# A first product with seven products of quarters in four of its blocks, and gating shared with GpSimd

## The chip, the cores and the metric

The kernel runs on one core of a Trainium2 chip. The metric is the device time of one execution in microseconds; the number given for a kernel is the median of its runs.

## What is computed

A recurrent attention (a decaying state per head) is followed by a two-layer network with a gated non-linearity. Cut to what matters:

```python
# q, k, v: (B=4, H=8, S=768, D=64)
for t in range(S):
    state = gamma * state + outer(k[:, :, t], v[:, :, t])
    y[:, :, t] = q[:, :, t] @ state / sqrt(D)
x = y.transpose(0, 2, 1, 3).reshape(B * S, H * D)      # 3072 tokens, 512 features
h = x @ w_in                                           # 512 -> 2048
g = maximum(h, 0) + alpha * minimum(h, 0)              # alpha: one number per feature of h
out = g @ w_out                                        # 2048 -> 512
```

## The kernel before

**Blocks and units.** The 3072 tokens are worked through in six blocks n of 512 tokens (`TB`), each of two units u of 256 (`U`). While block n is in the two products of the network, units 2(n+1) and 2(n+1)+1 of the next block go through the attention. Everything is issued in an order written out by hand; the products are generators, and `tick(gen, m)` issues the next m of their matmuls between pieces of attention. Each engine works through its queue in that order.

**First product** (`ffn1`, L591 to L604). 2048 features are 16 tiles of 128. In blocks 2 to 5 a tile is four matmuls over the 512 input features, with 512 tokens as columns, into one PSUM bank (`hps`); the 16 tiles go in turn through all eight banks. ScalarE writes `hm` = relu(-h) (L602), and VectorE gates, `gt` = hm * (1 - alpha) + h (L604), reading the bank a second time. In blocks 0 and 1 some tiles are done in halves of 256 tokens.

**Second product.** Block 0 is a plain product (`ffn2`, L629). In blocks 1 to 5 `ffn2_seven` (L677) cuts it into two by two quarters and does seven products of quarters in place of eight (16 matmuls of 256 columns each), with sums of quarters of `gt` (`g_sums`, L575, four per block on VectorE) and of `w_out` (`w_sums`, L562, once). One bank is seeded: ScalarE copies the first product's bank `ox` into `oy` (L699), and TensorE adds to it. The first two sums of `gt` are made in halves, one half-way through the first product and one at its end (in blocks 2 to 5; whole at its end in block 1).

**Attention in a block** (n = 1 in one form, n = 2 to 4 in another with halves of units). GpSimd scales k and q and casts them (`rescale`, L178) and casts v (`cast_v`, L194); these two `rescale`s and the cast per unit stand in the queue at the start of a block, the first of them held until the last `g_sums` of the block before (`gate`, `behind`). DMA transposes give `kq`. TensorE makes the states (`halves_mm`), the scores (`half_mm`), VectorE masks the scores (`half_masks`, L349), VectorE and GpSimd advance the state (`middle` L294, `behind_middle` L305/L306, with casts L326, L442), TensorE makes the output of the heads (`halves_out`, L377, L391), and ScalarE writes it as `xT` (`take_y`, L546), which is x of the next block.

Where the next block starts, VectorE's queue holds: the last `g_sums`, the addition for one store (`plus`, L703), the addition for the last store of the block (which reads bank 0), and then the gates of the next block.

Tiles that aren't persistent come from pools with 1 to 3 buffers under a tag.

Of the kernel before, what the change touches and what calls it, by code (L numbers as in the profile page):

```python
# [14 lines left out]
MULT = mybir.AluOpType.mult  # L15
ADD = mybir.AluOpType.add
# [5 lines left out]
def kernel(  # L22
# [61 lines left out]
    mj = sbp.tile([128, 512], F16, tag="mj", name="mj")[:, 0:384]  # L84
# [3 lines left out]
    warm = sbp.tile([128, 128], FP, tag="warm", name="warm")[:, 0:1]  # L88
    oma_sb = sbp.tile([128, 128], FP, tag="oma", name="oma")[:, 0:NFT]
# [4 lines left out]
    wsum = sbp.tile([128, 4, HF, HM], F16, tag="wsum", name="wsum")  # L94

    def ps(bank, name, dt=FP, n=512):
        return psp.tile([128, n], dt, tag=f"b{bank}", name=name)
# [11 lines left out]
    moved, mids = {}, {}  # L109
# [177 lines left out]
    def middle(u, c):  # L287

        s = sums.pop((u, c))
        m = sbp.tile([128, NP, 64], FP, tag="tm", bufs=2, name=f"tm{u}_{c}")  # L290
# [7 lines left out]
    def behind_middle(ucms):  # L298
# [4 lines left out]
        ss = sbp.tile([128, NP, 64], FP, tag="ss", bufs=2, name=f"ss{u}_{c}")  # L303
        t = sbp.tile([128, NP, 64], FP, tag="tf", bufs=3, name=f"tf{u}_{c}")
# [42 lines left out]
    def half_masks(u, a):  # L347
        m2 = sbp.tile([128, 512], F16, tag=f"m2{a}{u % 2}", bufs=2, name=f"m2{a}")
        nc.vector.tensor_tensor(  # L349
            out=m2.rearrange("p (x i) -> p x i", x=8),  # L350
            in0=live[u][a].rearrange("p (x i) -> p x i", x=8),
            in1=mj[:, 256:320].unsqueeze(1).to_broadcast([128, 8, 64]),
            op=MULT,
        )
        live[u][a] = m2
# [50 lines left out]
    def state_sum(u, c, eng):  # L406
# [3 lines left out]
        t = sbp.tile([128, NP, 64], FP, tag="tf", bufs=3, name=f"tf{u}_{c}")  # L410
        if u % UPB == 0 and c == 0:
            nc.vector.tensor_tensor(out=t, in0=s, in1=dec, op=MULT)
        else:
            ss = sbp.tile([128, NP, 64], FP, tag="ss", bufs=2, name=f"ss{u}_{c}")
# [50 lines left out]
    def masks(u, hh, parts=(0, 1)):  # L465
        for a in parts:
            m2 = sbp.tile([128, 512], F16, tag=f"m2{a}{hh}", bufs=2, name=f"m2{a}{hh}")
# [86 lines left out]
    def w_sums(i, lo, hi, eng=nc.vector):  # L554

        w = w_out_all.rearrange("p (k f) (j e) -> p k f j e", k=2, j=2)
        w12, w21, w22 = w[:, 0, lo:hi, 1, :], w[:, 1, lo:hi, 0, :], w[:, 1, lo:hi, 1, :]
        t1, t2, t3, t4 = (wsum[:, x, lo:hi, :] for x in range(4))
        o, a, b = (
            (t1, w12, w[:, 0, lo:hi, 0, :]), (t2, w22, t1), (t3, w22, w12), (t4, w21, t2)  # L560
        )[i]
        return eng.tensor_tensor(out=o, in0=a, in1=b, op=SUB)  # L562
# [14 lines left out]
    def ffn1(n, banks, apart=0):  # L577
# [9 lines left out]
        for i, (f0, nf, lo, hi) in enumerate(turns):  # L587
# [12 lines left out]
            hm = sbp.tile([128, TB], FP, tag="hm", bufs=3, name="hm")  # L600
# [18 lines left out]

    def ffn2(n, banks, parts=1):  # L620
# [3 lines left out]
        for f0 in range(0, NFT, step):  # L624
            for tq in range(4):
                if f0 == 0:
                    opss[tq] = ps(banks[tq % len(banks)], "ops")
                for ft in range(f0, f0 + step):
# [7 lines left out]
                    if ft == NFT - 1:  # L636
                        tag = ("os", "cu")[tq % 2]
                        os_sb = sbp.tile([128, d_model], FP, tag=tag, bufs=3, name=tag)
# [7 lines left out]
    def ffn2_seven(n, x, y, z=None):  # L646
# [16 lines left out]
        def ws(i):  # L663
            return lambda f: wsum[:, i, f, :]
# [7 lines left out]

        def product(o, lhs, rhs, first, after=None):

            for m in range(2):
                for f in range(HF):
# [4 lines left out]
                        start=(first and f == 0 and m == 0),  # L681
                        stop=(f == HF - 1),
                        skip_group_check=True,
                    )
                    if f == HF - 1 and after is not None:
                        after(m)
                    if m == 0 or f < HF - 1:
                        yield

        def kept(o, name="cu"):  # L690
            t = sbp.tile([128, 2, HM], FP, tag=name, bufs=3, name=name)
            moves((t, [t[:, 0, :], t[:, 1, :]]), o)
            return t

        def moves(o, i):

            whole = o[0] is not None and i[0] is not None
            for a, b in [(o[0], i[0])] if whole else zip(o[1], i[1]):
                nc.scalar.activation(out=a, in_=b, func=COPY, bias=0.0, scale=1.0)  # L699

        def plus(o, t, name="os"):
            so = sbp.tile([128, 2, HM], FP, tag=name, bufs=3, name=name)
# [3 lines left out]
        def store(i, j, t):  # L706
# [367 lines left out]
```

## Time and profile before

| | |
|---|---|
| median of three runs | 201.17 us (199.87 to 201.18) |
| the profiled execution | 199.25 us, span 197.4 us |
| TensorE busy, its matmuls | 190.0 us (96%), 2493 |
| VectorE / ScalarE / GpSimd busy | 148.9 / 115.2 / 93.6 us |
| granted TensorE clock | 1.00 |
| 16 DMA engines, mean rate | 176 GB/s |

Times in a trace are counted from the span's start. A row of a timeline or of the chain begins with the start and the duration in microseconds; a group's row ends with its total busy time, the mean of one in nanoseconds, and the engine's idle time before it with what ended that. PE is TensorE, DVE VectorE, ACT ScalarE, POOL GpSimd, SP the engine that issues most transfers. The chain is followed back from the last instruction: at each step to what released it. TensorE's records overlap (a matmul of 512 columns is shown as 379 ns and the next starts 216 ns after it), so its pace is read from the chain.

### The profile page before, as it was taken

How to read it: one execution, taken by the hardware profiler on the slowest of the kernel's cores; microseconds unless marked ns; L12 is line 12 of the kernel's file. 1: busy time of each engine (PE TensorE's matmuls, PEld its weight loads, DVE VectorE, ACT ScalarE, POOL GpSimd, SP SyncE). 2: the span in 40 equal slices, each digit the busy share in tenths (PEclk: the TensorE clock that was granted, in tenths of full speed). 3: DMA queues.
4: the chain of work that ended last, by engine and by line, in shares of the span. 5: the costliest groups of instructions: out<-in, count | busy, mean ns of one | idle time of the engine just before them, and what ended most of it. 6: DMA issues, size and time to landing. Idle time of an engine off the chain costs nothing.

```text
span 197.4 us, 5972 instructions
## 1 busy us (share of the span) xinstructions
PE 190.0 (96%) x2493; PEld 125.3 (64%) x2493; DVE 148.9 (75%) x243; ACT 115.2 (58%) x200; POOL 93.6 (47%) x107
## 2 busy tenths in 40 slices
PE   6788999999999999999999999999999999999993
PEld 2456544577477788644788544888544888445882
DVE  6896985527789996489986489985589993789821
ACT  3467675257286667466477476377466485566221
POOL 6288047399439374960187950268940370000000
PEclk9999999999999999999999999999999999999999
DMA  6999999999899979898895999948955011200014
GB/s 159 335 259 169 202 260 260 294 181 188 200 228 124 327 160 278 224 262 183 197 233 123 309 193 212 240 111 201 253 108 128 9 56 58 104 0 3 0 53 159
DMA packets 88185, 34.75 MB, mean 176 GB/s; under 512 B 57936, under 2 KB 87648, under 8 KB 88160
## 3 DMA queue, kind: packets, MB, share of 16 engines
q1 hardware_dynamic: 83760, 30.16, 62.3%
q0 software_dynamic: 4224, 4.19, 13.5%
q8 instruction: 19, 0.31, 0.7%
q10 hardware_dynamic: 176, 0.04, 0.2%
q14 instruction: 6, 0.05, 0.1%
HBM read 27.31 MB, written 6.29 MB: 170 GB/s over the span
## 4 chain that ended last, share of the span: by engine, by line
PE 90%; DMA 6%; SPq 1%; ACT 1%; POOL 0%; issue 0%; POOLq 0%
PE hps L591 42%; PE ox L677 16%; PE oy L677 14%; PE ops L629 7%; DMA win<-in_moe_w_in_dram 3%; DMA vs<-in_v_dram 3%; SPq L158 1%; PE y L523 1%; PE trb L223 1%; PE oz L677 1%; PE st L277 1%; PE sca L456 1%; PE y L377 1%; PE ow L677 1%; PE y L391 1%; PE y L491 1%
## 5 line engine op out<-in xcount | busy, mean ns | idle before, releaser
L591 PE MATMUL hps<-xT,win 128*128 128x512 f16 (+1 forms) x448 | 84.7, 349 | 0.3 <-DMA win<-in_moe_w_in_dram 0.3
L604 DVE SCALAR_TENSOR_TENSOR gt<-hm,oma,hps 128x512 f16<-128x512 f32 (+1 forms) x112 | 70.7, 668 | 15.2 <-ACT hm L602 10.1
L602 ACT ACTIVATE hm<-hps 128x512 f32<-128x512 f32 x96 | 57.0, 597 | 31.6 <-PE hps L591 28.8
L591 PEld LDWEIGHTS <-win 128*128 128x128 f16 x448 | 43.5, 98 | 38.9 <-DMA win<-in_moe_w_in_dram 0.5
L677 PEld LDWEIGHTS <-gs 128*128 128x128 f16 x320 | 30.9, 98 | 3.9 <-DVE gs L575 0.3
L677 PEld LDWEIGHTS <-gt 128*128 128x128 f16 x240 | 22.8, 98 | 4.5
L178 POOL TENSOR_TENSOR kdq<-ks,tab 128x1024 f16<-128x1024 f32 (+1 forms) x12 | 19.4, 1614 | 10.5 <-DMA ks<-in_k_dram 7.9
L178 POOL TENSOR_TENSOR kdq<-qs,tab 128x1024 f16<-128x1024 f32 (+1 forms) x13 | 20.4, 1571 | 3.3 <-DVE wsum L562 3.0
L326 POOL CAST tg<-tm 64x256 f16<-64x256 f32 x12 | 4.8, 398 | 33.9 <-DVE tm L294 22.5
L677 PE MATMUL ox<-wout,gt 128*128 128x256 f16 x160 | 19.3, 273 | 0.0
L677 PE MATMUL oy<-wsum,gs 128*128 128x256 f16 x160 | 19.1, 273 | 0.0
L546 ACT ACTIVATE xT<-y 128x512 f16<-128x512 f32 x23 | 15.7, 742 | 3.9 <-PE y L523 2.8
L703 DVE TENSOR_TENSOR os<-ox,cu 128x512 f32<-128x512 f32 x8 | 5.5, 692 | 13.4 <-PE ox L677 12.1
L629 PE MATMUL ops<-wout,gt 128*128 128x512 f16 x64 | 15.3, 380 | 0.0
L194 POOL CAST vx<-vs 128x1024 f16<-128x1024 f32 (+1 forms) x13 | 12.5, 973 | 3.9 <-DMA vs<-in_v_dram 3.9
L575 DVE TENSOR_TENSOR gs<-gt 128x1024 f16<-128x1024 f16 (+1 forms) x14 | 12.8, 918 | 0.3
L229 ACT ACTIVATE kq<-trb 128x1024 f16<-128x1024 f16 x8 | 8.2, 1023 | 6.5 <-PE trb L223 6.4
L306 POOL TENSOR_TENSOR tf<-ss,tab 128x256 f32<-128x256 f32 x10 | 10.3, 1030 | 2.5 <-DVE ss L305 1.3
L699 ACT ACTIVATE cu<-oy 128x512 f32<-128x512 f32 (+1 forms) x12 | 6.3, 526 | 8.3 <-PE oy L677 7.7
L416 POOL TENSOR_TENSOR tf<-ss,tab 128x256 f32<-128x256 f32 x8 | 6.5, 817 | 9.8 <-DVE ss L415 9.8
L677 PE MATMUL oy<-wsum,gt 128*128 128x256 f16 x80 | 9.5, 272 | 0.1
L629 PEld LDWEIGHTS <-gt 128*128 128x128 f16 x64 | 5.8, 98 | 6.0
(86 smaller groups left out, 213.6 us busy)
## 6 DMA issues: line engine op xcount, KB each, us to landing
out_dram<-os SPq DMA_DIRECT2D x21, 256.0 KB, 3.5
ks<-in_k_dram SPq DMA_DIRECT2D x32, 128.0 KB, 3.7
qs<-in_q_dram SPq DMA_DIRECT2D x8, 512.0 KB, 5.1
vs<-in_v_dram SPq DMA_DIRECT2D x32, 128.0 KB, 4.4
ks<-in_k_dram SPq DMA_DIRECT2D x8, 256.0 KB, 4.5
qs<-in_q_dram SPq DMA_DIRECT2D x8, 256.0 KB, 4.6
win<-in_moe_w_in_dram POOLq DMA_DIRECT2D x4, 512.0 KB, 6.6
wout<-in_moe_w_out_dram POOLq DMA_DIRECT2D x4, 512.0 KB, 6.5
```

The lines of the kernel that those rows point to most:

```text
L178: return eng.tensor_tensor(out=kdq[:, t, :, h0:h1, :].rearrange("p r h d -> p h r d"), in0=staged[u]["kq"[t]][:, h0:h1, :].rearrange("p h ...
L194: eng.tensor_copy(out=o, in_=i)
L229: nc.scalar.activation(out=kq.rearrange("p (x a) i -> p x a i", x=4)[:, :, 2 * hh : 2 * hh + 2, :], in_=trb.rearrange("p (x a i) -> p x a ...
L306: nc.gpsimd.tensor_tensor(out=t, in0=ss, in1=dec, op=MULT)
L416: eng.tensor_tensor(out=t, in0=ss, in1=dec, op=MULT)
L546: nc.scalar.activation(out=o, in_=i, func=COPY, bias=0.0, scale=1.0,)
L575: return nc.vector.tensor_tensor(out=o, in0=a, in1=b, op=op)
L591: nc.tensor.matmul(out=hps[:, f, :].rearrange("p (u t) -> p u t", t=U), lhsT=w_in_all[:, hp, 128 * (f0 + f) : 128 * (f0 + f) + 128], rhs=x ...
L602: nc.scalar.activation(out=hm, in_=hps, func=RELU, bias=0.0, scale=-1.0)
L604: nc.vector.scalar_tensor_tensor(out=gt[:, f0 + f, U * lo : U * hi], in0=hm[:, f, :], scalar=oma_sb[:, f0 + f : f0 + f + 1], in1=hps[:, f, :],
L629: nc.tensor.matmul(out=opss[tq], lhsT=gt[:, ft, 128 * tq : 128 * tq + 128], rhs=w_out_all[:, ft, :], start=(ft == 0), stop=(ft == NFT - 1),)
L677: nc.tensor.matmul(out=o[1][m], lhsT=lhs(f, m), rhs=rhs(f), start=(first and f == 0 and m == 0), stop=(f == HF - 1), skip_group_check=True,)
```

## The change

1. *Seven products in the first product.* In blocks 2 to 5, tiles 6, 7, 14 and 15 (a two by two cut of features, tokens and input features) are done by seven products of quarters, "steps" 1 to 7, each four matmuls of 256 columns: step 1 makes a product in banks 2 and 3, ScalarE copies it into banks 0 and 1 (the seed), steps 6, 7 and 4 add to the seed, steps 5 and 3 go to bank 4; after steps 6 and 7 ScalarE copies the seed out, and after 4 and 3 VectorE adds such a copy to bank 4 into PSUM, where the usual gate reads it. They need four sums of `w_in` (`in_sums`, once, on GpSimd, after block 1's attention) and four of x (`x_sums`, in each block, on VectorE, right after the attention of the block before).
2. *The order* of tiles and steps is the list `PLAN`, and the twelve plain tiles go mostly through banks 7, 6 and 5 in turn.
3. *GpSimd gates* tiles 3, 5, 8 and 11: ScalarE copies the bank, GpSimd makes min(h, 0) * (alpha - 1), then adds h. It also masks one of each block's four score tiles, which ScalarE copies first.
4. *Sums of gated tiles*: the first two are made whole, after all tiles. Sum 3 is made earlier in the attention's order.
5. *Sums of w_out*: the first is made in place of a quarter of `w_out`, by VectorE, after block 0's second product; before, by GpSimd into a buffer of its own.
6. *Last block*: the seven products of the second product come in another order, with one more bank; what ends last is a VectorE addition of 128x256 in two halves, and two stores go out from ScalarE's queue.
7. *Buffers*: PSUM is one tile cut by bank, some pools become rings in fixed turn, masks have one buffer in place of two.

The core of the diff:

```diff
+    def x_sums(n, eng):
+        xs = sbp.tile([128, 4, 2, U], F16, tag="xs", name=f"xs{n}")
+        b11, b21, b12, b22 = (xT[n][:, ul, 2 * k : 2 * k + 2, :] for ul in range(2) for k in range(2))
+        t1, t2, t3, t4 = (xs[:, i] for i in range(4))
+        for o, a, b in ((t1, b12, b11), (t2, b22, t1), (t3, b22, b12), (t4, b21, t2)):
+            eng.tensor_tensor(out=o, in0=a, in1=b, op=SUB)
...
+    def prelu_pool(n, f, hps):
+        h = ring([128, TB], "hm", 4, "hm")
+        nc.scalar.activation(out=h, in_=hps, func=COPY, bias=0.0, scale=1.0)
+        m = sbp.tile([128, TB], FP, tag="hn", bufs=1, name="hn")
+        nc.gpsimd.tensor_scalar(
+            out=m, in0=h, scalar1=0.0, scalar2=al_sb[:, f : f + 1], op0=MIN, op1=MULT
+        )
+        nc.gpsimd.tensor_tensor(out=gts[n][:, f, :], in0=h, in1=m, op=ADD)
...
+    def ffn1_mixed(n, plan, banks, pool=()):
...
+            o, lhs, rhs, start = {
+                1: (f11, w(0, 0), x(0, 0), True),
+                2: (f11, w(1, 0), x(1, 0), False),
+                3: (bv, wi[:, 3], x(1, 1), False),
+                4: (g21, w(1, 1), xs[:, 3], False),
+                5: (bv, wi[:, 0], xs[:, 0], True),
+                6: (g21, wi[:, 1], xs[:, 1], False),
+                7: (g21, wi[:, 2], xs[:, 2], False),
+            }[i]
...
+            if i == 1:
+                nc.scalar.activation(out=g21, in_=f11, func=COPY, bias=0.0, scale=1.0)
+            elif i in (6, 7):
+                t = ring([128, 2, HM], "cu", 3, "cu")
+                nc.scalar.activation(out=t, in_=g21, func=COPY, bias=0.0, scale=1.0)
+                sums[f, i] = t
+            elif i in (3, 4):
+                o = (bf if i == 3 else bg)
+                nc.vector.tensor_tensor(
+                    out=o[:, :, U : 2 * U], in0=bv, in1=sums.pop((f, 6 if i == 3 else 7)), op=ADD
+                )
...
-    def half_masks(u, a):
+    def half_masks(u, a, eng=nc.vector):
...
+        if eng is nc.gpsimd:
+            nc.scalar.activation(out=m2, in_=i, func=COPY, bias=0.0, scale=1.0)
+            i = m2
...
-    w_sums(0, 0, HF, G)
...
+    w_sums(0, 0, HF)
     tick(half)
+    a = steps(6, 2, 0, 4)
+    PLAN = [0, 1, a[1], a[5], 2, a[6], a[2], 3, a[7], 4, a[4], 5, 8, a[3], 9, 10, 11, 12, 13]
+    PBANKS = (7, 6, 5, 7, 6, 5, 7, 6, 5, 1, 7, 4)
+    POOLED = (3, 5, 8, 11)
...
-            gen = ffn1(n, (7, 2, 3, 1, 0, 6, 5, 4, 7, 1, 0, 4, 5, 6, 7, 1))
+            gen = ffn1_mixed(n, *((PLAN, PBANKS, POOLED) if more else (PLAN, PBANKS, POOLED)))
...
             tick(gen)
+            g_sums(n, 0, GS if more else 0, HF)
+            g_sums(n, 1, GS if more else 0, HF)
...
             half_mm(u0, (4, 5))
+            half_masks(u0, 1, G)
             m00 = middle(u0, 0)
...
-            tick(gen, 9)
-            half_masks(u0, 1)
+            tick(gen, 1)
+            g_sums(n, 2, 0, HF)
             m10 = middle(u1, 0)
...
             halves_out(u1, (4, 5))
             state_copy(s11, part=1)
+            x_sums(n + 1, V)
...
             out_mm(u0 + 1, (4, 5))
+            for i in range(4):
+                in_sums(6, i, G)
+            x_sums(n + 1, V)
```

228 lines of the change are left out of this document (170 added, 58 removed).

## The prediction

> **What bounds the kernel now.** I read the page's engine shares first, then the chain of work that ended last, then the groups with shapes kept apart, then the timeline where one block ends and the next begins.
>
> ```profile
> PE 190.0 (96%) x2493; PEld 125.3 (64%) x2493; DVE 148.9 (75%) x243; ACT 115.2 (58%) x200; POOL 93.6 (47%) x107
> PEclk9999999999999999999999999999999999999999
> ```
>
> TensorE is busy for 96% of the span at full clock. The others have time to spare, so they matter only where TensorE waits for them. The chain through block 2 and into block 3:
>
> ```profile
> 80.85 13.81 PE hps L591 x64
> 94.67 1.79 PE ox L677 x16
> ...
> 99.36 1.75 PE oy L677 x16
> ...
> 101.98 0.27 PE y L377 x17
> ...
> 109.97 13.81 PE hps L591 x64
> ```
>
> A block takes 109.97 - 80.85 = 29.12 us and is TensorE from end to end. The first product is 64 matmuls of 512 columns in 13.81 us, 0.2158 us each. A product of quarters is 16 matmuls of 256 columns in 1.75 us, 0.109 us each. Any gain must come from fewer columns; any wait that TensorE meets is a loss at full price.
>
> **The change part by part.**
>
> *Columns.* In blocks 2 to 5 four of the 16 tiles (16 matmuls, 16 x 0.2158 = 3.45 us) become seven products of four matmuls of 256 columns (28 x 0.109 = 3.06 us). That is -0.39 us per block, -1.6 us over four. Bounds: at half of a 512-column matmul, 0.108 us, it is -0.43; at the first row of a product above, 1.79 us / 16 = 0.112, it is -0.32. I take -0.39.
>
> *What replaces it on the other engines.* The durations:
>
> ```profile
> L604 DVE SCALAR_TENSOR_TENSOR gt<-hm,oma,hps 128x512 f16<-128x512 f32 x80 | 57.6, 745 | 8.4 <-ACT hm L602 3.2
> L602 ACT ACTIVATE hm<-hps 128x512 f32<-128x512 f32 x96 | 57.0, 597 | 31.6 <-PE hps L591 28.8 <-DVE gt L604 2.2
> L575 DVE TENSOR_TENSOR gs<-gt 128x2048 f16<-128x2048 f16 x6 | 7.3, 1220 | 0.0
> L575 DVE TENSOR_TENSOR gs<-gt 128x1024 f16<-128x1024 f16 x8 | 5.5, 691 | 0.3
> L699 ACT ACTIVATE oy<-ox 128x512 f32<-128x512 f32 x4 | 2.3, 582 | 4.7 <-PE ox L677 4.7
> L703 DVE TENSOR_TENSOR os<-ox,cu 128x512 f32<-128x512 f32 x8 | 5.5, 692 | 13.4 <-PE ox L677 12.1 <-ACT cu L699 1.2
> L178 POOL TENSOR_TENSOR kdq<-qs,tab 128x512 f16<-128x512 f32 x5 | 5.2, 1046 | 0.0
> L194 POOL CAST vx<-vs 128x512 f16<-128x512 f32 x2 | 1.2, 622 | 0.0
> L326 POOL CAST tg<-tm 64x256 f16<-64x256 f32 x12 | 4.8, 398 | 33.9 <-DVE tm L294 22.5 <-DVE tm L292 10.9
> L294 DVE TENSOR_TENSOR tm<-tf,st 128x256 f32<-128x256 f32 x10 | 4.2, 416 | 1.0 <-POOL tf L306 1.0
> ```
>
> ScalarE goes from 16 evictions to 19 in a first product of 13.4 us: 19 x 0.6 = 11.4 us, which fits but leaves the last tiles queued. VectorE goes from 16 gates to 12 plus two additions. An addition that writes PSUM isn't in the trace; bounds 0.69 (L703) and 0.75 (the gate, also with a PSUM input); I take 0.69. That is 14 x 0.69 = 9.7 us, less than before. GpSimd gets four tiles, each a two-step scalar operation and an addition of 512. The addition is like L178 at 512, 1.05 us. The scalar operation isn't in the trace: from 0.62 (the cast) to 1.05 (two inputs); it has one input tensor, so I take 0.65. The Trainium skill (GPSIMD Engine Reference, 4.1 Engine selection) says that one-input operations run at about line rate there and two-input ones about twice as slow as on VectorE; by it too the lower end would be right. So 1.7 us per tile (up to 2.1), 6.8 us (up to 8.4).
>
> I place these in the order of the plan, with time 0 at the first matmul of the block: tiles 0 and 1 end at 0.86 and 1.73, step 1 at 2.16, step 5 at 2.60, tile 2 at 3.46, and step 6 may then start. If VectorE is free, nothing stalls but step 4/3 (0.1 us, VectorE's addition must read bank 4 before step 3 writes it). The first two sums of gated tiles (2 x 1.22) now wait for all 16 tiles: from tile 5's copy at 8.1 on, ScalarE has eleven evictions in a row (6.6 us) with 0.35 of waits, to 15.1; the last gate follows to 15.85, which is 2.4 us after TensorE leaves the first product (13.45), and the sums end 4.8 us after; the product that reads them starts 99.36 - 94.67 = 4.69 us after. Cost +0.1 (bounds 0 and +0.9).
>
> *The mask on GpSimd.* ScalarE copies (0.6), GpSimd multiplies (about 1.05, as L178 at 512). It stands ahead of the state work in GpSimd's queue (cast, decay, casts) and needs the port which those two sums hold. From the end of the first product: the two sums end at 4.8, mask to 5.85, cast (0.40) to 6.25, decay (0.61) to 6.86, VectorE's next state (0.42) to 7.28, its cast (0.40) to 7.7, with the gaps between them 7.85. The output product of the heads, which reads that cast, began at 101.98 - 94.67 = 7.3, and now 0.1 later. Cost +0.4 in blocks 2 to 4 (bounds 0, if the mask gets in between the two sums at no loss to them, and +1.0, if it holds the second up by its 1.05).
>
> *The four sums of x on VectorE.* This decides. They are 512 elements of fp16, two SBUF inputs; by the rows of 1024 and 2048 (0.53 per 1024) about 0.69 - 0.27 = 0.42 us. They stand in VectorE's queue ahead of the addition for the last store (L703) and of all gates of the next block. In the trace before, VectorE and GpSimd shut each other out when both have two SBUF inputs:
>
> ```profile
> 12.00 0.68 DVE L178 TENSOR_TENSOR kdq<-ks,tab 128x512 f16<-128x512 f32 x1
> 12.16 1.00 POOL L416 TENSOR_TENSOR tf<-ss,tab 128x256 f32<-128x256 f32 x1 [0.50 <-DVE ss L415]
> 12.61 1.10 DVE L178 TENSOR_TENSOR kdq<-qs,tab 128x512 f16<-128x512 f32 x1
> ```
>
> and again, and at last GpSimd's operation alone:
>
> ```profile
> 54.06 0.69 DVE L562 TENSOR_TENSOR wsum<-wout,wsum 128x1024 f16<-128x1024 f16 x1
> 54.22 1.00 POOL L416 TENSOR_TENSOR tf<-ss,tab 128x256 f32<-128x256 f32 x1 [0.22 <-DVE ss L415]
> 54.66 1.10 DVE L562 TENSOR_TENSOR wsum<-wout 128x1024 f16<-128x1024 f16 x1
> ```
>
> ```profile
> 98.47 0.61 POOL L306 TENSOR_TENSOR tf<-ss,tab 128x256 f32<-128x256 f32 x1
> ```
>
> Twice the same figure: GpSimd's decay comes while VectorE works and takes 1.00 us, though 0.61 where it is alone (98.47); then VectorE's next takes 1.10 for 0.69. They take turns, one whole instruction each, even where VectorE's two don't depend on each other. Here the turns of GpSimd are long. The border of blocks 2 and 3:
>
> ```profile
> 106.38 1.34 ACT L546 ACTIVATE xT<-y 128x512 f16<-128x512 f32 x2
> 106.97 1.90 POOL L178 TENSOR_TENSOR kdq<-ks,tab 128x1024 f16<-128x1024 f32 x1
> 108.83 1.90 POOL L178 TENSOR_TENSOR kdq<-qs,tab 128x1024 f16<-128x1024 f32 x1
> 110.01 0.69 DVE L703 TENSOR_TENSOR os<-ox,cu 128x512 f32<-128x512 f32 x1 [3.02 <-PE ox L677]
> 110.68 1.03 POOL L194 CAST vx<-vs 128x1024 f16<-128x1024 f32 x1
> 111.51 6.79 DVE L604 SCALAR_TENSOR_TENSOR gt<-hm,oma,hps 128x512 f16<-128x512 f32 x8 [0.80 <-ACT hm L602]
> 111.67 1.90 POOL L178 TENSOR_TENSOR kdq<-ks,tab 128x1024 f16<-128x1024 f32 x1
> ...
> 115.38 1.03 POOL L194 CAST vx<-vs 128x1024 f16<-128x1024 f32 x1
> ```
>
> x is whole at 106.38 + 1.34 = 107.72; GpSimd has begun its first rescale at 106.97, and the rescales aren't moved. (The gates in this stretch have an input in PSUM, and the rescales beside them keep 1.90, so gates don't collide.) By turns: first sum 108.75 to 109.15, rescale to 110.95, second sum to 111.3, cast to 112.2, third to 112.6, rescale to 114.4, fourth to 114.8, the store's addition (0.69) to 115.5. That is 5.5 us after 109.97; it stood at 0.7. What is late next: the addition reads bank 0, and ScalarE's seeding copy of step 1 writes it, so the copy (0.58) ends at 6.1; ScalarE's queue stands behind it, and step 6 waits from 3.46 to 6.1: **+2.65 us**. The gates, 5.5 us late, free banks 7, 6 and 5 in time for TensorE so delayed. Bounds: 0 if the addition ends by 2.85 (then the copy ends before 3.46), and +3.1 with an addition at 5.9 (each turn without overlap at its ends). Blocks 2, 3 and 4 begin so; before block 5 GpSimd has no rescale.
>
> *Costs nothing.* The first weight sum moves from GpSimd to VectorE (1.22), ahead of block 1's last gates:
>
> ```profile
> 68.26 1.23 DVE L575 TENSOR_TENSOR gs<-gs,gt 128x2048 f16<-128x2048 f16 x1
> ```
>
> ```profile
> 70.12 1.75 PE oy L677 x16
> ```
>
> Those gates and two sums end at 69.49, and the product that reads them starts at 70.12, so 0.6 of it is hidden and the rest is little; with a turn lost to a rescale it is +1.9, once. The four sums of w_in (about 1.05 each) run on GpSimd once, where it waits for the next rescale. Fixed turns of buffers, one tile for PSUM and single mask buffers keep the order in which readers end before writers, which TensorE's own order covers; without it a mask of 0.69 us per unit would show. The last block ends as before: a VectorE addition of 256 for a ScalarE copy of 256, then the same store.
>
> *Sum.* Blocks 2 to 4: -0.39 + 0.1 + 0.1 + 0.4 + 2.65 = +2.85 each, +8.55; block 5: -0.39 + 0.1 = -0.3. Together +8.25. The profiled execution took 199.25 us (span 197.4); the median of the runs shown is 201.17, 1.9 above it and the profiled one below the lowest of them. So 207.5 to 209.4; I say 208.5.
>
> **The rivals.**
>
> *The sums slip through (no loss).* Place: the same border. If VectorE's four sums go one behind another with at most one rescale between, the addition ends by 2.85 and step 6 doesn't wait. For it: the third sum needs nothing of the second and can follow at once, and GpSimd may come to its rescale later than in the old trace, since the mask and the casts ahead of it do. Against it: both pairs of rows above, and 106.97 lies 0.75 ahead of 107.72. Then blocks 2 to 4 cost -0.39 + 0.1 + 0.1 + 0.4 = +0.2 each, total +0.3: 201.4. If the sums and the mask cost nothing too, -0.39 x 4 = -1.6: 199.6, or 199.1 with the 0.108 us matmul and a run level as low as the lowest shown.
>
> *GpSimd becomes the bound.* For it: its rescales and casts end at 116.4, 6.4 us into the block, and turns given to VectorE move that to 8; the four tiles follow at up to 2.1 us, to 16.4, and the two sums wait for them, where VectorE's own last gate ends at 13.4 + 2.4 = 15.8. Against it: the cast of 512 at 0.62. That is +0.6, and ScalarE's buffers that it holds make it about +1, in three blocks over the case before: 204.5.
>
> *The wait lowers TensorE's clock.*
>
> ```profile
> L591 PE MATMUL hps<-xT,win 128*128 128x512 f16 x320 | 70.0, 379 | 0.0
> L102 PE MATMUL kps<-spin 128*128 128x512 f16 x20 | 6.5, 462 | 1.5 <-DVE spin L788 1.5
> ```
>
> The first matmuls of the kernel take 462 ns, later ones 379, so TensorE does have a slower start. Should 2.65 us of idling bring it back, I put one product (1.75 us) twice as long: +1.75 in three blocks, 213.8. The page's clock row shows no drop anywhere. The Trainium skill (TensorE: Matmul & The Clock Gate, HAM oscillation) warns of idle gaps over about 3.4 us; by that rule the wait forecast here is just too short, and no run here shows one.
>
> **How the numbers follow.** The turns as forecast, with one or more of their waits shortened: 0.52, 208.5, own range 204.5 to 211. GpSimd the bound: 0.08. The clock: 0.04. No loss: 0.36, of which the part below 199.2 is 0.13. So faster by over 1%: 0.13; within 1%: 0.24; slower by over 1%: 0.63. One per cent, 2 us, is about what a measurement of this kernel can tell from no change: three runs lie 1.3 us apart. The range from 198.8 to 211.5 leaves about 0.1 out at each end.
>
> **What would show it.** Right: the four sums of x on VectorE at 1 to 2 us from start to start in blocks 2 to 4 and at about 0.4 before block 5; a TensorE wait of 2 to 3 us on ScalarE between tile 2 and step 6 in three blocks; the first product at about 16 us there and 13.5 in block 5. Wrong: the sums back to back, and first products of 13.5 us in all four.

## The result, and the profile after

| | before | after |
|---|---|---|
| median of four runs | 200.52 us (199.65 to 201.18) | 246.3 us (245.1 to 248.87) |
| ratio | 1 | 1.2266, 95% interval 1.2169 to 1.2363 |
| profiled execution, its span | 199.25, 197.4 us | 245.1, 243.3 us |
| granted TensorE clock | 1.00 | 0.944 |

Some executions run in a slower state at a lower clock (here the one of 248.87 us, below the one of 229.26 us of `e2_vgate`); ratios and the differences formed below leave them out. So the change costs some 45 us (245.63, the median of the other three, less 200.52); the forecast was 208.5, with 211.5 as its upper end. The page's shares and clock row of the changed kernel, then the start of its chain's summary:

```profile
PE 204.9 (84%) x2541; PEld 135.0 (55%) x2541; DVE 171.3 (70%) x243; ACT 119.6 (49%) x211; POOL 153.4 (63%) x146
PEclk9999999999999999979997997998599589999799
...
PE 38%; POOL 25%; DVE 13%; issue 9%; ACT 4%; DMA 4%; SPq 4%; POOLq 0%; ACTq 0%; DVEq 0%
```

TensorE is down from 96% to 84%, a quarter of the chain is GpSimd's, and the clock, flat before, falls in block after block. The groups that the prediction priced:

```profile
L672 POOL TENSOR_SCALAR hn<-hm,oma 128x512 f32<-128x512 f32 x16 | 31.9, 1994 | 29.4 <-ACT hm L670 28.6
L675 POOL TENSOR_TENSOR gt<-hm,hn 128x512 f16<-128x512 f32 x16 | 20.2, 1265 | 1.3
L609 DVE TENSOR_TENSOR xs<-xT 128x512 f16<-128x512 f16 x8 | 22.7, 2837 | 2.9 <-ACT xT L563 2.9
```

GpSimd's scalar operation takes 1.994 us (0.65 in the sum), its addition 1.265 (1.05). The last row holds the two sums of x in four that read x alone: they should take 0.42 each and have a mean of 2.837. The timeline at the border of blocks 2 and 3, VectorE and GpSimd, and TensorE behind them:

```profile
118.09 0.39 POOL L459 CAST th<-tf 64x256 f16<-64x256 f32 x1
118.44 1.90 POOL L191 TENSOR_TENSOR kdq<-ks,tab 128x1024 f16<-128x1024 f32 x1
118.46 9.70 DVE L609 TENSOR_TENSOR xs<-xT 128x512 f16<-128x512 f16 x1 [0.31 <-ACT xT L563]
...
126.85 1.03 POOL L207 CAST vx<-vs 128x1024 f16<-128x1024 f32 x1
128.20 0.42 DVE L609 TENSOR_TENSOR xs<-xT,xs 128x512 f16<-128x512 f16 x1
128.22 1.01 PE L748 MATMUL psum<-xs,wi 128*128 128x256 f16 x4 [5.42 <-DVE xs L609]
```

VectorE's first sum begins with the first of GpSimd's six queued operations and ends only after the last of them (126.85 + 1.03 = 127.88): no turns at all, and GpSimd is not slowed by it (1.90, as alone). The other three sums then take 0.42 each. TensorE waits 5.42 us. At the border of blocks 1 and 2 the same four sums do take turns, as forecast (the third and the fourth):

```profile
81.11 2.08 POOL L191 TENSOR_TENSOR kdq<-ks,tab 128x1024 f16<-128x1024 f32 x1
81.36 2.12 DVE L609 TENSOR_TENSOR xs<-xT 128x512 f16<-128x512 f16 x1
83.16 2.08 POOL L191 TENSOR_TENSOR kdq<-qs,tab 128x1024 f16<-128x1024 f32 x1
83.40 2.12 DVE L609 TENSOR_TENSOR xs<-xT,xs 128x512 f16<-128x512 f16 x1
86.87 0.60 PE L748 MATMUL psum<-xs,wi 128*128 128x256 f16 x4 [1.73 <-ACT psum L759]
```

Here TensorE waits 1.73 us for ScalarE's seeding copy, the wait that was priced at 2.65.

### The profile page after: what moved, and what is told of

Its sections match the earlier page's. It is cut to its first block, busy times and chain, and to the rows that moved or that the text cites. A ratio compares the mean times of both kernels' runs of the same rounds, so it can differ in the third digit from the quotient of the medians.

```text
span 243.3 us, 6166 instructions
## 1 busy us (share of the span) xinstructions
PE 204.9 (84%) x2541; PEld 135.0 (55%) x2541; DVE 171.3 (70%) x243; ACT 119.6 (49%) x211; POOL 153.4 (63%) x146
## 4 chain that ended last, share of the span: by engine, by line
PE 38%; POOL 25%; DVE 13%; issue 9%; ACT 4%; DMA 4%; SPq 4%; POOLq 0%; ACTq 0%; DVEq 0%
PE psum L834 16%; PE psum L638 10%; POOL hn L672 10%; POOL gt L675 6%; POOL kdq L191 5%; PE psum L784 4%; DVE gt L684 3%; DMA vs<-in_v_dram 3%; DVE gs L622 3%; SPq L165 2%; POOL vx L207 2%; PE psum L703 2%; DVE xs L609 2%; DVE wsum L579 2%; PE psum L748 1%
## 5 line engine op out<-in xcount | busy, mean ns | idle before, releaser
L684 DVE SCALAR_TENSOR_TENSOR gt<-hm,oma,psum 128x512 f16<-128x512 f32 x48 | 34.3, 745 | 33.0 <-ACT hm L682 32.9
L672 POOL TENSOR_SCALAR hn<-hm,oma 128x512 f32<-128x512 f32 x16 | 31.9, 1994 | 29.4 <-ACT hm L670 28.6
L703 PE MATMUL psum<-xT,win 128*128 128x512 f16 x192 | 48.0, 393 | 1.5 <-DVE gt L684 1.5
L682 ACT ACTIVATE hm<-psum 128x512 f32<-128x512 f32 x48 | 27.4, 599 | 31.0 <-POOL gt L675 18.8
L651 DVE SCALAR_TENSOR_TENSOR gt<-hm,oma,psum 128x256 f16<-128x256 f32 (+1 forms) x48 | 24.9, 567 | 7.3 <-ACT hm L649 5.9
L834 PE MATMUL psum<-wout,gt 128*128 128x256 f16 x160 | 25.1, 308 | 5.4 <-DVE gt L684 4.3
L638 PE MATMUL psum<-xT,win 128*128 128x256 f16 (+1 forms) x192 | 28.9, 308 | 0.5 <-DVE gt L651 0.3
L609 DVE TENSOR_TENSOR xs<-xT 128x512 f16<-128x512 f16 x8 | 22.7, 2837 | 2.9 <-ACT xT L563 2.9
L649 ACT ACTIVATE hm<-psum 128x512 f32<-128x512 f32 x32 | 18.9, 596 | 8.2 <-PE psum L638 6.8
L675 POOL TENSOR_TENSOR gt<-hm,hn 128x512 f16<-128x512 f32 x16 | 20.2, 1265 | 1.3
L834 PE MATMUL psum<-wout,gs 128*128 128x256 f16 x160 | 19.8, 273 | 0.0
```

What stands on the lines that cost most here:

```text
L638: nc.tensor.matmul(out=hps[:, f, :].rearrange("p (u t) -> p u t", t=U), lhsT=w_in_all[:, hp, 128 * (f0 + f) : 128 * (f0 + f) + 128], rhs=x ...
L649: nc.scalar.activation(out=hm, in_=hps, func=RELU, bias=0.0, scale=-1.0)
L651: nc.vector.scalar_tensor_tensor(out=gt[:, f0 + f, U * lo : U * hi], in0=hm[:, f, :], scalar=oma_sb[:, f0 + f : f0 + f + 1], in1=hps[:, f, :],
L672: nc.gpsimd.tensor_scalar(out=m, in0=h, scalar1=0.0, scalar2=al_sb[:, f : f + 1], op0=MIN, op1=MULT)
L675: nc.gpsimd.tensor_tensor(out=gts[n][:, f, :], in0=h, in1=m, op=ADD)
L682: nc.scalar.activation(out=hm, in_=hps, func=RELU, bias=0.0, scale=-1.0)
```

## The experiments

Theory Q: VectorE's sums of x wait for GpSimd's whole queue, and GpSimd's gates are a loss of their own. Theory G: GpSimd's gates take too long, everything that needs tile 11 waits for them, and that is nearly all of the loss. Theory P (the port): the wait of the sums at the borders is nearly all of it. Rivals besides: the late sums, the clock by itself.

**1. Parts taken out of the changed kernel.** `e1_hold` holds the next block's rescales until the last sum of x:

```diff
-            x_sums(n + 1, V)
+            gate = x_sums(n + 1, V)
```

> The changed kernel with one edit: GpSimd's first rescale for the next block is held until the last of the four sums of x (before, until the last sum of gated tiles). Theory Q (a VectorE sum that meets GpSimd's queue at the port waits until that whole queue has run dry, 9.7 us, and GpSimd's 3.4 us per gated tile is a loss of its own): the sums take 0.42 us each in all blocks, the stall in front of step 5 or 6 goes, first products still end late by GpSimd's tiles; blocks 2 to 4 take about 35 us each and the kernel 226 to 230. Theory G (GpSimd's gating is nearly all of the loss, and what waits for the sums would wait for GpSimd anyway): 240 or more. Theory P (the port is nearly all): 203 to 208.

`e2_vgate` has `POOLED = ()`: VectorE gates all tiles.

> The changed kernel with VectorE gating all 16 tiles; the port at the border is left as it is. Theory Q: blocks 3 and 4 still lose 6 to 7 us each to the sums of x and block 2 about 3; block 5 is within 1 us of before; 217 to 223. Theory G: 203 to 208. Theory P: above 235.

`e3_both` has both edits.

> Both edits: the rescales held behind the sums of x, and VectorE gates all 16 tiles. What is left of the change: seven products, sums of x, the late sums of gated tiles, the mask on GpSimd, buffers. By the hand schedule the two sums of gated tiles end 5.9 us after the first product (4.7 is needed), which gives back what the columns save: 203 to 207, and a granted clock of 1.00 again. If instead a third cause is at work (PSUM as one tile, the rings), above 212.

`e4_both_vmask` has, besides, `half_masks(u0, 1)` on VectorE again.

> As the run with both edits, and the mask that GpSimd makes goes back to VectorE. If the mask on GpSimd costs the 0.4 us per block that the prediction gave it, 1 us below the run with both edits; if VectorE is by now what is late, the same or 1 us above it.

| | median, us | ratio to before | clock |
|---|---|---|---|
| changed kernel | 246.3 | 1.2266 [1.2169, 1.2363] | 0.944 |
| rescales held | 238.07 | 1.1829 [1.1697, 1.196] | 0.96 |
| VectorE gates | 223.93 (one run) | | 0.975 |
| both | 211.14 | 1.0455 [1.0349, 1.0561] | 1.00 |
| both, mask on VectorE | 210.44 | 1.0481 [1.0385, 1.0577] | 0.997 |

Both causes are there, so neither G nor P is right, and their losses don't simply add: GpSimd's gates cost 245.63 - 223.93 = 21.7 us in the kernel as it is and 26.9 with the rescales held; holding gains 7.6 or 12.8. Q named the causes but priced them too low: the first run lies 8 us over its range, the second 1, and the third between its range and the 212 above which a third cause was to be looked for. Whoever makes the mask, the time is the same as far as these runs can tell. Some 4.5% are left without either.

**2. Parts alone, put into the kernel before.** `f1_pool_alone`: in blocks 2 to 5 tiles 3, 5, 8 and 11 are gated by GpSimd.

> The kernel before, with its plain first product; in blocks 2 to 5 GpSimd gates tiles 3, 5, 8 and 11 as in the changed kernel, and nothing else is changed. Theory Q (3.4 us per tile, in a queue that starts after the rescales): VectorE's first half of the sums waits for tile 11 until about 17 us into the block, so blocks 2 to 4 lose about 7 us each and block 5 about 3: 222 to 228. If GpSimd's gating were dear only together with the seven products: 201 to 206.

`f2_xsums_alone`: four sums of x that nothing reads, on VectorE in the change's place.

> The kernel before, with the four sums of x on VectorE at the place where the changed kernel has them; nothing reads them (two of them share a buffer). Theory Q (the first sum waits until GpSimd's queue of rescales and casts has run dry): it lasts 8 to 9 us at the borders of blocks 2/3 and 3/4, the addition for the last store ends about 7 us into the block, and the kernel is at 205 to 209. Theory of turns (the prediction's): each sum waits for one rescale, the addition ends at 5.5 us, 203 to 206. If the port cost nothing: 201 to 202.

`f3_late_alone`: the first two sums of gated tiles whole, after all tiles.

```diff
-            if n > 0 and f0 in ((HF + 3, NFT - 1) if apart == 0 else (NFT - 1,)):
+            if n > 0 and f0 == NFT - 1:
```

> The kernel before, with the first two sums of gated tiles made whole after all 16 tiles in blocks 2 to 5 too (they were made in halves). The sums end 1.4 + 2.4 = 3.9 us after the first product, ahead of the 4.7 that are needed; what follows on VectorE is 1 us later and has about 1 us of slack: 200.5 to 202.5. If this edit is what leaves the run with both edits 10 us behind: above 205.

`f4_xsums_held`: as `f2_xsums_alone`, with the rescales held until the last sum.

> The kernel before with four unused sums of x, as in the run that added them alone (217.24 us against 199.5), but the first rescale of GpSimd held until the last of the four. Theory, the sums lose their time only because GpSimd's queue of rescales is ahead of them: the four take 0.42 us each, TensorE meets no wait over 1 us at the blocks' borders, and the time is 200.5 to 203. Rival, four operations ahead of the store's addition and the gates cost it by themselves, or the rescales that now begin some 2 us later do: 205 to 212.

Measured: 242.37 (1.2146 [1.2021, 1.2271]), 217.24 (1.0886 [1.0804, 1.0969]), 204.29 (1.0235 [1.0153, 1.0317]) and 202.27 (1.0115 [1.0006, 1.0223]). The first three lie above what the theories gave them, the fourth as forecast. In `f2_xsums_alone` the first sum takes 9.02 us at the border of blocks 2 and 3 and 9.01 at the next, and TensorE waits 5.38 us behind each. The sums of x alone cost 17.7 us, and holding the rescales takes 15.4 of that away: it is the queue, not the sums. GpSimd's gates alone cost more than the whole theory gave them, because the kernel before makes its first sums half-way through the first product, in VectorE's queue ahead of other gates. Two rows of the waits of `f1_pool_alone`:

```profile
DVE gs L577 <- POOL gt L609: 34.8, 4, 9.4
PE hps L593 <- DVE gt L620: 26.6, 4, 7.4
```

VectorE stands 9.4 us at a sum that needs GpSimd's tile, the gates behind it aren't made, and TensorE has no free bank. The change's own later sums avoid this, so the 43 us here overstate what these gates cost in the change. In `f3_late_alone` VectorE's state work of block 2 begins at 98.84 us, in the kernel before at 97.45:

```profile
98.84 0.42 DVE L292 COPY tm<-st 128x256 f32<-128x256 f32 x1
```

```profile
97.45 0.42 DVE L292 COPY tm<-st 128x256 f32<-128x256 f32 x1
```

That is 1.39 us, of which 0.16 is an earlier shift (the second product starts at 94.83 and 94.67). TensorE meets it as a wait for a copy of ScalarE, which stands in its queue behind copies of the state; the row gives the sum, the times and the longest:

```profile
PE ox L676 <- ACT os L698: 2.3, 3, 0.8
```

By its ratio the run costs some 1.2 us in each of four blocks.

**3. What GpSimd's operation costs.** `b1_port`, a bench, runs its forms alone, and then lets VectorE meet six queued operations.

> A bench, not the computation: the outputs are zeros. First GpSimd's operations of 512 elements one after another with the port to themselves: two-step scalar operation with a scalar from memory, one step with an immediate, one step from memory, two steps with immediates, additions to fp32, to fp16, of fp16, a copy. Expected: two steps with a scalar from memory 2.0 us, one step less than half of that if the steps are what costs, additions 1.05 to 1.27. Then five meetings at the port, each with six operations of 1024 in GpSimd's queue and four of 512 on VectorE, VectorE coming in the first of GpSimd's. Theory Q: in case 1 (GpSimd's six independent) VectorE's first lasts 9 to 11 us, until GpSimd's queue is dry; in case 2 (each of GpSimd's waits for the one before) it gets in after one; in case 3 (VectorE in hand first) they take turns; case 4 (VectorE with one input, 16 bit) like 1 if the mode needs the port; case 5 (GpSimd with one input) like 1. Theory of turns: one operation's wait in all five.

Groups of the bench with shapes kept apart (L79 is the gate's form; L81 min with a constant; L83 multiplication by a number per row; L85 multiplication and addition with constants; L93 a copy):

```profile
L79 POOL TENSOR_SCALAR r<-x,al 128x512 f32<-128x512 f32 x3 | 6.0, 1995 | 0.1
L83 POOL TENSOR_SCALAR r<-x,al 128x512 f32<-128x512 f32 x3 | 4.7, 1561 | 0.0
L81 POOL TENSOR_SCALAR r<-x 128x512 f32<-128x512 f32 x3 | 4.4, 1484 | 0.0
L85 POOL TENSOR_SCALAR r<-x 128x512 f32<-128x512 f32 x3 | 1.8, 618 | 0.0
L93 POOL COPY r<-x 128x512 f32<-128x512 f32 x3 | 1.7, 610 | 0.0
```

Here, where VectorE only fills buffers beside it, the form takes 1.995 us, as in the kernel: no contention, the operation itself. Only the copy and the form with two constants run near the 0.65 that the prediction took; a number per row makes it 1.56, a minimum 1.48. `g1_light` lets ScalarE write the second half, so that GpSimd only adds (on top of `e1_hold`):

```diff
-        nc.gpsimd.tensor_scalar(
-            out=m, in0=h, scalar1=0.0, scalar2=al_sb[:, f : f + 1], op0=MIN, op1=MULT
-        )
+        nc.scalar.activation(out=m, in_=hps, func=RELU, bias=0.0, scale=al_sb[:, f : f + 1])
```

> The changed kernel with the rescales held until the last sum of x (238.07 us), and in the four tiles that GpSimd gates ScalarE now writes the second half too (relu of h times alpha - 1, a second read of the bank), so that GpSimd only adds: 1.27 us a tile in place of some 3.4, 5.1 in place of 13.6 a block. Theory, what GpSimd's gating costs is the length of its queue behind the rescales: 207 to 213, near the 211.1 of VectorE gating all. Rival, it costs by its place (tiles of a third engine in ScalarE's ring, and four more copies on ScalarE, 23 x 0.6 = 13.8 us in a first product of 13.5): over 222.

Measured: 216.95 (1.0858 [1.0768, 1.0948]), 21.1 us below `e1_hold`. It lies between the two forecasts, some 6 us over VectorE gating all (8 by the ratios): most of the loss was the length of GpSimd's operation. That the rest is the place (a copy more in ScalarE's queue per tile, and a gate that comes later) is argued; no run shows it alone.

**4. Turns or the whole queue.** `b2_turns`, a bench:

> A bench, no part of the computation, outputs are zeros: GpSimd has six operations in its queue (two rescales and a cast, twice), VectorE comes with four subtractions of 512 fp16, three times with the rescales in the kernel's own form (its views, a table spread over 64), early (0.2 us), in the middle (0.8) and late (1.5 us) in the first rescale, and twice (early, late) with plain rows in place of the views. Theory A, the phase decides: early and middle arrivals wait until all six have ended (about 9 us, as at two borders in the changed kernel), a late one gets turns of one operation each. Theory B, the form decides: the kernel's rescales never let VectorE in (9 us in all three), plain rows give turns (about 2 us from start to start). If all five give turns, the cause of the long wait in the kernel stays open.

All five cases took turns, like the five meetings of the bench before, for which theory Q had expected waits of 9 to 11 us: neither theory held. What the kernel has and the benches had not is a cast on rows 0 to 63 that runs directly ahead of the six (118.09 above). `b4_rows` puts one there:

> A bench, no part of the computation, outputs are zeros: the six operations of GpSimd and the four subtractions of VectorE as in the bench before, VectorE some 0.7 us into the first rescale; directly ahead of the six stands a cast of 256 elements in rows 0 to 63 (as in the kernel), in all 128 rows, in rows 64 to 127, in rows 0 to 63 with a short cast of 128 rows behind it, and in rows 0 to 63 with idle time behind it. Theory, an operation on half of the partitions directly ahead lets the halves of GpSimd run apart, and then no gap between its operations lets VectorE in until it runs dry: cases 1 and 3 wait some 8 to 9 us for the first subtraction, case 4 too, cases 2 and 5 take turns (2.1 us from start to start). Rival, rows have nothing to do with it: all five take turns.

The timeline of its first case (rows 0 to 63), then of its second (all rows):

```profile
17.82 0.39 POOL L113 CAST tg<-y 64x256 f16<-64x256 f32 x1 [0.28 <-DVE tg L136]
18.18 3.75 POOL L83 TENSOR_TENSOR kd<-st,tab 128x1024 f16<-128x1024 f32 x2
18.54 9.36 DVE L121 TENSOR_TENSOR s<-h,d 128x512 f16<-128x512 f16 x1 [0.79 <-ACT d L119]
...
28.93 0.39 POOL L113 CAST tg<-y 128x256 f16<-128x256 f32 x1
29.29 3.94 POOL L83 TENSOR_TENSOR kd<-st,tab 128x1024 f16<-128x1024 f32 x2
29.76 1.71 DVE L121 TENSOR_TENSOR s<-h,d 128x512 f16<-128x512 f16 x1 [0.85 <-ACT d L119]
```

9.36 us against 1.71. The other three cases gave turns too (1.72, 1.73 and 1.84 us): a cast on rows 64 to 127, a short one of all rows in between, idle time in between. So half of the theory holds (case 1, and cases 2 and 5) and half does not (3 and 4). In case 1 the next operation starts 0.03 us before the cast's end (17.82 + 0.39), in case 3 0.08 after it:

```profile
40.08 0.40 POOL L113 CAST tg<-y 64x256 f16<-64x256 f32 x1
40.56 3.94 POOL L83 TENSOR_TENSOR kd<-st,tab 128x1024 f16<-128x1024 f32 x2
```

In case 2 it also starts 0.03 us before the cast's end (28.93 + 0.39), and turns follow, so such an overlap alone is not the cause. Whether case 3 differs from case 1 by its gap or by its rows is open. In the kernel itself, `k1_th_scalar` (on top of `f2_xsums_alone`) moves that cast to ScalarE:

```diff
-            state_copy(s11, part=0)
+            state_copy(s11, copy="aa", part=0)
             gate = g_sums(n, 3, 0, HF)
```

> The kernel before with four unused sums of x (217.24 us), but the cast of half of the partitions that GpSimd makes directly ahead of the next block's rescales goes to ScalarE. Theory, as for the bench: the sums take turns with the rescales as the prediction had it, about 2 us from start to start at all three borders, and the time falls to 203 to 208. Rival: the first sum waits some 9 us at two borders as before, 215 to 219.

Measured: 207.83 (1.0386 [1.0312, 1.0459]). The border of blocks 2 and 3 now:

```profile
110.06 1.82 DVE L572 TENSOR_TENSOR xs<-xT 128x512 f16<-128x512 f16 x1 [0.53 <-ACT xT L546]
111.92 1.14 DVE L572 TENSOR_TENSOR xs<-xT,xs 128x512 f16<-128x512 f16 x1
113.09 2.01 DVE L572 TENSOR_TENSOR xs<-xT 128x512 f16<-128x512 f16 x1
115.14 2.00 DVE L572 TENSOR_TENSOR xs<-xT,xs 128x512 f16<-128x512 f16 x1
```

With one cast of 0.39 us on another engine, the sums take turns at all three borders, and the run costs 3.9% in place of 8.9%. Not all of that is the turns. Two rows of its waits:

```profile
PE hps L602 <- DVE os L714: 4.5, 3, 1.8
PE oy L688 <- ACT cu L710: 2.6, 2, 1.4
```

TensorE waits 4.5 us for the stores' additions, which stand behind the sums, and 2.6 for a copy of ScalarE behind the moved cast, which waits there for GpSimd's state.

**5. The clock.** `b3_clock`, a bench:

> A bench, no part of the computation, outputs are zeros: TensorE runs 100 matmuls of 512 columns (some 21.6 us), and then six times 72 (15.5 us), each stretch behind a wait of about 1.9, 3, 4.2, 5.4, 6.6 and 8.4 us for ScalarE. Theory, a wait of over some 4 us lowers the granted clock for the stretch behind it (0.83 to 0.93 in windows of the changed kernel behind waits of 4.2 and 5.4 us), a shorter one does not: 1.00 behind the first two, below 0.95 behind the last three. Rival, the clock fell for another cause (the load of all engines together): 1.00 everywhere here.

TensorE's timeline, 72 matmuls behind each wait:

```profile
29.14 15.70 PE L60 MATMUL b<-r,w 128*128 128x512 f16 x72 [2.01 <-ACT r L69]
48.23 17.39 PE L60 MATMUL b<-r,w 128*128 128x512 f16 x72 [3.39 <-ACT r L69]
70.33 17.11 PE L60 MATMUL b<-r,w 128*128 128x512 f16 x72 [4.71 <-ACT r L69]
93.47 17.48 PE L60 MATMUL b<-r,w 128*128 128x512 f16 x72 [6.03 <-ACT r L69]
118.31 17.01 PE L60 MATMUL b<-r,w 128*128 128x512 f16 x72 [7.36 <-ACT r L69]
144.66 17.48 PE L60 MATMUL b<-r,w 128*128 128x512 f16 x72 [9.34 <-ACT r L69]
```

A wait of 2.01 us costs nothing behind it; each of the five of 3.39 or more costs 1.3 to 1.8 us, however long it is. The theory had the bound at some 4 us; it lies lower. The clock in windows of the bench (PEclk is the third number from the end), behind the first and the fourth wait:

```profile
29.20:33.00 3.80, 3.80 (x18) 1.70 (x18) 0.00 (x0) 0.00 (x0) 0.00 (x0) 1.00 0.00 0
93.60:97.00 3.40, 3.40 (x9) 1.18 (x8) 0.00 (x0) 0.00 (x0) 0.00 (x0) 0.50 0.00 0
```

Half clock for some 3 us, with no other engine at work behind the wait: a wait is enough. The bench puts the bound between 2.01 and 3.39 us, and the kernels' traces show that it is not sharp: of the four waits of 2.62 us in `h3_order` (below) three are followed by a lower clock (the 16 matmuls behind them take 3.39, 2.75 and 2.45 us, behind the fourth 1.91), and of the four of 2.42 us in `h1_order` and in `h2_order` one each. The Trainium skill (TensorE: Matmul & The Clock Gate, HAM oscillation) gives idle gaps over about 3.4 us as the bound; the bench alone is in line with that, the waits of 2.62 us are not, and the measurement decides.

**6. A better order.** Without GpSimd's gates and with held rescales the chain of waits runs, at the end of each first product, through VectorE's last gates and the two sums. Three of its pieces in `e4_both_vmask`, start, duration and what, where TensorE leaves the first product at 126.42:

```profile
125.74 4.05 DVE gt L685 x6
129.82 1.24 DVE gs L623
131.08 1.23 DVE gs L623
```

`h1_order` moves the steps of the seven products forward (on top of `e4_both_vmask`):

```diff
-    PLAN = [0, 1, a[1], a[5], 2, a[6], a[2], 3, a[7], 4, a[4], 5, 8, a[3], 9, 10, 11, 12, 13]
+    PLAN = [a[1], 1, 2, a[6], 3, a[5], a[7], 4, a[4], 5, 13, a[2], a[3], 11, 10, 12, 8, 9, 0]
```

> The changed kernel with the rescales held until the last sum of x, all tiles gated by VectorE and all score tiles masked by it (210.44 us so far), and the steps of the seven products earlier in the order of tiles, so that the last gates and the two sums end about 4.8 us after the first product in place of some 6. Theory, what is left over the kernel before is that lateness (about 1 us a block, by the run that only made the sums late) and the held rescales (about 2.5 in all, by the run with held sums): 202 to 206. Rival, the seven products cost by themselves what is left: 208 to 212.

It took 223.57 us; its tile 5 overwrites tile 14 in bank 0 (this part of the result is changed) and ties the gates to each other, so the time tells nothing. `h2_order` puts tile 5 into bank 6:

> As the run with another order of the steps, with tile 5 in bank 6 in place of bank 0, which tile 14 had not left there. By a hand schedule of a block the first product has 0.1 us of waits and its sums are ready 4.8 us behind it, against 5.5 by the same schedule for the order of the change. Theory, what is left over the kernel before is the lateness of the sums and the held rescales: 203 to 207. Rival, the seven products cost what is left by themselves (more work in VectorE's and ScalarE's queues than they take out): 208 to 212.

214.63 (1.0683 [1.0621, 1.0745]), above both ranges: tile 0 is last, the second product reads it first, and TensorE waits 2.42 us for it in each of four blocks. `h3_order` changes the order once more:

> As the run with the order of the steps changed (214.63 us), in an order that also has tiles 0 to 7 gated by the time the second product reads them (tiles 13, 11 and 9 last). By the hand schedule 0.05 us of waits in the first product, sums ready 4.84 us behind it, against 5.46 in the order of the change: 0.6 to 0.7 us a block less than the 210.44 of that order. Theory, lateness of the sums is what is left: 203 to 208. Rival, the seven products cost what is left by themselves: 208 to 212.

213.95 (1.0672 [1.0636, 1.0708]), with tiles 13, 11 and 9 last. The last one sat in bank 0, which the second product writes first; TensorE waited again, and the granted clock was 0.50 behind the wait:

```profile
98.37 3.39 PE L835 MATMUL psum<-wout,gt 128*128 128x256 f16 x16 [2.62 <-DVE gt L685]
```

`h4_order` has the last three in banks 5, 7 and 4:

```diff
-    PBANKS = (7, 6, 5, 7, 6, 5, 7, 6, 1, 7, 6, 0)
+    PBANKS = (7, 6, 5, 7, 6, 5, 7, 6, 1, 5, 7, 4)
```

> As the run before (213.95 us), with the last three tiles of the first product in banks 5, 7 and 4 in place of 7, 6 and 0, so that the second product, which writes bank 0 first, waits for none of the last gates. Theory, lateness of the sums is what is left over the kernel before, and this order takes some 0.6 us of it per block: 203 to 208. Rival, the seven products cost what is left by themselves (210.44 in the order of the change): 208 to 212.

208.95 (1.0357 [1.0285, 1.0429]). It is 1.5 us below the order of the change by the medians and 2.5 by the ratios, whose intervals overlap; it misses the theory's range by 1 us and lies in the rival's. In its trace the two sums end 5.3 us behind the first product, against 131.08 + 1.23 - 126.42 = 5.9 in `e4_both_vmask`: the 0.6 us a block that the theory priced did come, and most of the loss stayed. No variant of the change beats the kernel before.

## Why the prediction was wrong, point by point

The direction held, the size did not: some 45 us against 8.

- **GpSimd's gate, the largest miss: the sum had it hidden at no cost, because its operation was mis-sized.** "It has one input tensor, so I take 0.65", bounds 0.62 to 1.05; it took 1.994, and alone on the chip 1.995. Both bounds were rows of other operations (a cast, a two-input multiplication), and the true price lies outside. A tile takes 1.994 + 1.265 = 3.26 us in place of 1.7, four of them 13.0 in place of 6.8, and "GpSimd becomes the bound" (chance 0.08, 204.5) was what happened, at a price of 21.7 us. The step that failed is the price of the operation: the rival's condition was right, its row wrong. The rule quoted there (the Trainium skill, GPSIMD Engine Reference, 4.1 Engine selection, one-input operations at about line rate) fits the copy (0.610) and the form with constants (0.618), not this form; the measurement decides.
- **Turns: the mechanism was right where it applied, but it applied at one border in three.** There TensorE waited 1.73 us in place of 2.65. With turns at all borders (`k1_th_scalar`) the run cost a ratio of 1.0386, about 7.7 us on 200; that the sum had 3 x 2.65 = 7.95 is luck, since the turns' own waits there are 4.5 us and the moved cast's 2.6. In the change itself two of the three borders had the whole queue, and TensorE waited 5.42 and 4.20 us. The step that failed is the inference from the two pairs of rows to this queue. Its length alone is not what differs, for six queued operations took turns in the benches; the cast on half of the rows directly ahead is. The prediction read the queue but not what stood ahead of it.
- **The late sums, +0.1, were mis-sized.** They end 5.9 us behind the first product (`e4_both_vmask`) in place of 4.8, and the prediction timed them only against the product that reads them, though VectorE's state work stands behind them in its queue. In the kernel before the two sums end 96.84 + 0.69 - 94.67 = 2.9 us behind the first product:

```profile
96.84 0.69 DVE L575 TENSOR_TENSOR gs<-gs,gt 128x1024 f16<-128x1024 f16 x1
```

In the run that made only them late they end 1.2 us later than that, at a cost of 1.2 a block; in `e4_both_vmask` they end 3.0 later, in `h4_order` 2.4. So lateness may be most of what those two runs lose; no run shows that by itself.
- **The mask, +0.4, came at its upper bound of 1.0 as a wait, and at nothing in the time.** In `e3_both` GpSimd's mask gets in between the two sums; the second takes 2.20 us in place of 1.23, and TensorE waits for it in three blocks:

```profile
131.62 2.20 DVE L623 TENSOR_TENSOR gs<-gs,gt 128x2048 f16<-128x2048 f16 x1
PE psum L835 <- DVE gs L623: 3.6, 3, 1.2
```

With the mask on VectorE these waits are 0.23 us each, but the time is the same (1.0481 against 1.0455): what is won there is lost elsewhere, and where is not shown.
- **The clock, chance 0.04.** Its price was right (1.75 per wait in the prediction, 1.3 to 1.8 in the bench), its chance too small. The waits came out longer, and even one of 2.65, as forecast, would have been at risk by the waits of 2.62 above; the rule of 3.4 us that the prediction set against it does not hold for them. At a mean clock of 0.944 over 243.3 us, 243.3 x 0.056 = 13.6 us of full-speed time were withheld: an upper end for the clock's share of the loss.
- **The columns were right.** In `e4_both_vmask` the first product runs from 112.93 to 126.42, 13.49 us, against 13.81 - 0.39 = 13.42 (in the change itself block 5's takes 13.57, from 206.14 to 219.71):

```profile
112.93 1.89 PE L704 MATMUL psum<-xT,win 128*128 128x512 f16 x8
...
126.42 1.94 PE L835 MATMUL psum<-wout,gt 128*128 128x256 f16 x16
```

- **"Costs nothing"** (rings, one PSUM tile, sums of weights, the end) was not tested part by part. With the parts above taken out 3.6% stay (`h4_order`); the four sums of x with the rescales held cost about 1.2% by themselves (`f4_xsums_held`). Of the 7.5 us between the spans of `h4_order` and the kernel before, 1.1 lie ahead of block 2, 4.6 in blocks 2 to 4 and 1.8 from block 5 on. One part of the last is in the traces: the kernel does not end as before. The last operation ahead of the last stores, first before, then in `h4_order`:

```profile
194.17 0.38 ACT os L763
```

```profile
200.32 0.42 DVE cu L921
```

From its end to the end of the span it is 197.4 - 194.55 = 2.85 us and 204.9 - 200.74 = 4.16 us, 1.3 more. What the rest divides into is not settled.

Of the signs that the prediction named, three came: sums in turns at the first border, 0.4 us each ahead of block 5, and a first product of 13.5 there. The TensorE wait on ScalarE came in one block in place of three, at 1.73 us in place of 2 to 3. What would have told of the miss beforehand was not in its list: the row of the scalar operation itself, which no trace of before had.

## What to carry to other kernels

Bounds from the nearest rows hold only for the same form of operation: a price outside them is possible, and where an idle engine is to take 16 tiles, such an operation should be priced as unknown upwards too. Work that needs two SBUF inputs on VectorE should stand ahead of GpSimd's queue or be held apart from it by a dependency: here one line took 15.4 of 17.7 us away. And a sum that is late for the product that reads it is late, too, for everything behind it in its engine's queue.

## What the hardware showed

- VectorE's operation with two SBUF inputs can wait for six queued operations of GpSimd (up to 9.7 us in the kernels, 9.36 in the bench), and took turns of one operation each in the other cases (1.1 to 2.5 us, by the length of GpSimd's operation). Shown to decide: a cast on rows 0 to 63 directly ahead of the six, with no gap (`b4_rows`, `k1_th_scalar`). Why is open.
- GpSimd's scalar operation on 512 fp32 takes 0.618 us with two constants, 1.48 for a minimum, 1.56 with a number per row, 1.995 for both.
- The granted clock fell to 0.5 for about 3 us behind each TensorE wait of 3.39 to 9.34 us in the bench, and not behind one of 2.01; the price, 1.3 to 1.8 us, did not grow with the wait. In the kernels it fell behind three of four waits of 2.62 us and two of eight of 2.42.
